# Two layers of Fourier mixing and a spatial-shift MLP: chunk 3's z cast in two halves at later steps, the turns around it moved by one step, and one PSUM copy put ahead of a cast

## The chip, the cores and the metric

The kernel runs on one core of a Trainium2 chip. The metric is device time in microseconds; the kernel before was run three times, and the median counts. A profile of one further execution is read beside it.

The core has a matmul engine (TensorE, PE in the profile, with PEld its weight loads), a vector engine (VectorE, DVE), a scalar engine (ScalarE, ACT), GpSimd (POOL) and SyncE (SP), which in this kernel issues all transfers between HBM and the on-chip memory. Each engine takes its own instructions in the order in which the program emits them, and waits on semaphores for the others. Matmul results land in PSUM, eight banks of 128 x 512 fp32, here named PA, PB, PC and PD with two banks each (psa to psd in the profile).

## The reference

Two layers, each a block A and a block B on x of 2048 x 512, fp32:

```python
def _A_ref(x, dft_seq_re, dft_seq_im, dft_hid_re, dft_hid_im):
    a = jnp.einsum("bsd,ed->bse", x, dft_hid_re)
    b = jnp.einsum("bsd,ed->bse", x, dft_hid_im)
    y = jnp.einsum("ts,bse->bte", dft_seq_re, a) - jnp.einsum("ts,bse->bte", dft_seq_im, b)
    return y

def _B_ref(x, w1, w2, w3, w4):
    h = _gelu(_layernorm(x, axis=-1) @ w1)
    ...
    hs = jnp.concatenate([g0, g1, g2, g3], axis=-1) @ w2
    x1 = x + hs
    h2 = _gelu(_layernorm(x1, axis=-1) @ w3) @ w4
    return x1 + h2

x = x + _A_ref(_layernorm(x, axis=-1), ...)
x = x + _B_ref(_layernorm(x, axis=-1), ...)
```

g0 to g3 are the four quarters of h's columns, shifted along the sequence by +1, -1, +2 and -2 rows.

## The kernel before

**Split numbers.** Every matmul operand is kept as two fp32r numbers, a high part and a low part. `high` (L425) is a ScalarE cast of the fp32 value into the high part, `low` (L428) a VectorE subtraction of the high part from the value. One product of two split operands is three matmuls (`mm3`, L281 to L284): high x high, then the same left side with the right side's low part, then the left side's low part with the right side's high part. So the second or third matmul of a triple can need a low part that the first does not.

**Block A.** The sequence transform goes by chunks c of 512 output rows (four of them); `x_phase` (L475) and `y_phase` (L503) sum the products with the sequence matrices over eight pairs of row tiles. The matrices stream through four raw buffers and a ring of four split buffers: `stage_one` (L215) casts on ScalarE (L228, or L231 and L235 after a subtraction on VectorE), `stage_two` (L239) makes the low part on VectorE (L245). At the last `by1` block of the y phase PC and PD are complete; VectorE makes im0's value from PC (L517) and im1's from re0 and im0 (L520, shown as L468, the line of the helper `add`), ScalarE casts im0 (`high`, L426) and copies PD into X1 (L523). Two blocks of products into PB and PA follow, whose results are copied out at L531 and L533. In the last chunk they go to the tile `beside`, and the hidden transform (`hid`, L550) follows at once in the order of HORDER: its first product takes im0, and its accumulators are PC and PB (`acc4`). For the first three chunks the hidden products are spread over the next chunk's x phase.

**Block B.** `by_pairs` (L714) runs a list of 32 steps, each 12 matmuls of 128 x 128 by 128 x 512. `shifted(c, g)` (L643) multiplies chunk c's transposed normalised rows z (tile zt, halves 0 and 1 over the 512 hidden columns, `z_half`, L711) with column group g of w1; ScalarE applies the gelu into gt (L655) and casts the shifted view into rg (L658, the high part), and VectorE makes its low part (L659). `mixed(c, q)` (L668) multiplies the four groups of rg for one row tile with w2, group order 1, 3, 0, 2, and VectorE adds the result to the tile u (L677). Results rotate through the four banks PD and PA. The steps around the change:

| step | work | step | work |
|---|---|---|---|
| 15, 16, 17 | shifted, chunk 2, groups 1, 3, 0 | 23, 24, 25 | shifted, chunk 3, groups 1, 3, 0 |
| 18 | mixed, chunk 1, tile 3 | 26 | mixed, chunk 2, tile 3 |
| 19 | shifted, chunk 2, group 2 | 27 | shifted, chunk 3, group 2 |
| 20, 21, 22 | mixed, chunk 2, tiles 0 to 2 | 28 to 31 | mixed, chunk 3, tiles 0 to 3 |

**Side work by hand.** All other work of block B is hung on these steps by a schedule written out in the code. `D(n, ...)` puts work behind step n's matmuls and ahead of the step's own ScalarE and VectorE work; `A(n, ...)` puts it behind all of step n (`run`, L735). Within one place the order is that of the calls. A `norm` or `norm3` is a ScalarE normalisation (L330), `ln1_of` another one (four for each chunk, on A of steps 8c+3 to 8c+6, put there first, L844 to L846), `u_stats` the row statistics (VectorE L296 to L300 and two small GpSimd operations), `add_u` a VectorE addition, `turn` and `turn3` 32 x 32 block transposes on VectorE (L594).

To transpose a chunk, its four tiles are turned into a scratch tile (sc0, sc1, sc2), written to HBM by four transfers (`turn_out`, L596) and read back in another view: `turn_in` (L606) brings z into ztf, `b_in` (L696, called by `bring`) brings halves of the second transposed tensor z3d into the blocks "11", "21", "12", "22". The differences of these blocks (`sum_of`), their casts (`highs`) and low parts (`lows`) are operands of the last part of the block, which starts after step 31. Chunk 3's z is read back at A(16) and cast at A(18); its halves' low parts are made at D(21) and D(22). Chunk 1's second turn fills sc2 at D(20) and D(21), is written out at A(21) and read back at A(23); the sum at D(26) is the first use of block "12".

Of the kernel before, what the change touches and what calls it, by code (L numbers as in the profile page):

```python
# [14 lines left out]
S, D, F = 2048, 512, 1376  # L15
# [28 lines left out]
def spectral_mlp_kernel(ctx: ExitStack, tc: tile.TileContext, x, ws, hs, w1, w2, w34, out):  # L44
# [15 lines left out]
    z3d = [dram.tile([D, CH], F32, name=f"z3d{i}") for i in range(NC)]  # L60
# [63 lines left out]
    def xt(j):  # L124
        return xs[j // 2][:, j % 2]
# [29 lines left out]
    def y_order():  # L155
        order = [(k, kind) for k in range(NP) for kind in ("by1", "by0")]
        order[-3], order[-2] = order[-2], order[-3]
        return order
# [111 lines left out]
    def stream():  # L270
        i = state["use"]
        if i and items[i - 1][3] is None:
            state["done"] += 1
        state["use"] += 1
        prefetch()
        while state["two"] <= i:
            stage_two()
        return slots.pop(i)
# [137 lines left out]
    def mm_half(ps, a, slot, first, last):  # L416
        for i in range(2):
            w = slice(i * P, (i + 1) * P)
            mm3(ps[i], a[:, 0, w], a[:, 1, w], slot[:, 0], slot[:, 1], first, last)
# [5 lines left out]
    def high(tf):  # L425
        nc.scalar.copy(tf[0][:, :, 0], tf[1][:, :, 1])  # L426

    def low(tf):  # L428
        nc.vector.tensor_tensor(tf[0][:, :, 1], tf[1][:, :, 1], tf[0][:, :, 0].bitcast(F32), op=ALU.subtract)
# [37 lines left out]
    def add(o, a, b, op=ALU.add):  # L467
        nc.vector.tensor_tensor(o, a, b, op=op)  # L468

    def run_late(*names):  # L470
        for i in names:
            for f in late.pop(i, ()):
                f()
# [29 lines left out]
    def y_phase(c, hook):  # L503
        for k, kind in y_order():
            first, last = k == 0, k == NP - 1
            s = stream()
            if kind == "by1":
                hook(k)
                if k == 2:
                    run_late("y")  # L510
                if k == 4:
                    add(re0s, re0s, im1s)
                mm_half(PC, ay[k][:, 2], s[:, 0], first, last)
                mm_half(PD, ay[k][:, 0], s[:, 1], first, last)
                if last:
                    for i in range(2):
                        nc.vector.scalar_tensor_tensor(  # L517
                            im0s[:, i], PC[i], -1.0, im1s[:, i], op0=ALU.mult, op1=ALU.subtract
                        )
                    add(im1s, re0s, im0s)  # L520
                    high(im0)
                    for i in range(2):
                        nc.scalar.copy(X1[:, i], PD[i])  # L523
            else:
                if k == NP - 2:
                    low(im0)
                mm_half(PB, ay[k][:, 3], s[:, 1], first, last)
                mm_half(PA, ay[k][:, 1], s[:, 0], first, last)
        t = tmp if c < NC - 1 else beside
        for i in range(2):  # L530
            nc.scalar.copy(t[:, i], PB[i])  # L531
        for i in range(2):
            nc.scalar.copy(t[:, 2 + i], PA[i])  # L533
        late.update(
            {
                "im1-": [lambda: add(im1s, im1s, re1s, ALU.subtract)],
                "re1+": [lambda: add(re1s, re1s, t[:, 0:2]), lambda: high(re1)],
                "im1+": [lambda: add(im1s, im1s, X1), lambda: high(im1)],
                "re1": [lambda: low(re1)],
                "re0+": [lambda: add(re0s, re0s, t[:, 0:2])],  # L540
                "im1": [lambda: low(im1)],
                "re0++": [lambda: add(re0s, re0s, t[:, 2:4]), lambda: high(re0)],
                "re0": [lambda: low(re0)],
            }
        )
        if c < NC - 1:
            for i, names in enumerate((["im1-"], ["re1+"], ["im1+", "re1"], ["re0+", "im1"], ["re0++"], ["re0"])):
                late[i + 1] = [f for n in names for f in late.pop(n)]
# [43 lines left out]
    def turn_one(t, q, u):  # L592
        v = t.rearrange("p d (a q j) -> p d a q j", a=NB, q=TC)[:, :, :, q]
        nc.vector.transpose(v, blocks_of(u))  # L594

    def turn_out(t, to=None):  # L596

        if to is None:
            count["turn"] += 1
            to = zd[count["turn"] % 2]  # L600
        z = to.rearrange("(e i) t -> i e t", i=B)
        for b in range(NB):
            v = t[b * B : (b + 1) * B].rearrange("i d (a t) -> i (d a) t", a=NB)
            nc.sync.dma_start(z[:, :, b * P : (b + 1) * P], v)

    def turn_in(dst):  # L606

        z = zd[count["turn"] % 2].rearrange("(d p) t -> p d t", p=P)
        nc.sync.dma_start(dst[:, :, 1], z)
# [86 lines left out]
    def b_in(c, half, to):  # L696
        nc.sync.dma_start(blkf[to][:, :, 1], z3d[c].rearrange("(h d p) t -> h p d t", h=2, p=P)[half])
# [13 lines left out]
    def z_half(c, i):  # L711
        return [t[c % 2][:, 2 * i : 2 * i + 2] for t in (zt, ztf)]

    def by_pairs(layer, zs, xin, dst):  # L714
# [14 lines left out]
        def D(slot, *fs):  # L729
            todo.setdefault((slot, 0), []).extend(fs)  # L730

        def A(slot, *fs):
            todo.setdefault((slot, 1), []).extend(fs)
# [5 lines left out]
        def u_stats(c, i, n=2):  # L739
            return lambda: mrs[c].extend(stats(x1s[c][i : i + n]))  # L740

        def add_u(c, *qs):
            return lambda: [add(xt(c * TC + q), xt(c * TC + q), x1s[c][q]) for q in qs]

        def norm3(c, *qs):
            return lambda: [normed_act(x1s[c][q], x1s[c][q], mrs[c][q]) for q in qs]
# [10 lines left out]
        def turn3(t, c, *qs):  # L757
            return lambda: [turn_one(t, q, x1s[c][q]) for q in qs]
# [4 lines left out]
        def bring(c, half, to):  # L763
            return lambda: b_in(c, half, to)
# [13 lines left out]
        def z_highs(c):  # L778
            return lambda: [high(z_half(c, i)) for i in range(2)]
# [63 lines left out]
        sc0, sc1, sc2 = scratch  # L843
# [27 lines left out]
        D(14, turn(sc1, 3, 2, 3))  # L871
        A(14, lambda: turn_out(sc1))
        A(16, lambda: turn_in(ztf[1]))
        A(18, z_highs(3))
        D(21, lambda: low(z_half(3, 0)))
        D(22, lambda: low(z_half(3, 1)))

        D(6, u_stats(0, 0))
# [15 lines left out]
        D(18, add_u(1, 0, 1, 2))  # L894
        A(19, norm3(1, 0, 1, 2))
        D(19, u_stats(1, 3, 1))
        D(20, add_u(1, 3))
        D(20, turn3(sc2, 1, 0, 1, 2))
        A(20, norm3(1, 3))
        D(21, turn3(sc2, 1, 3))  # L900
        A(21, lambda: turn_out(sc2, z3d[1]))
        A(23, bring(1, 0, "12"), bring(1, 1, "22"))
        A(26, bring(0, 1, "t4"))
        D(26, sum_of("t1", "12", "t1"))
        A(27, highs("12", "22"))
# [538 lines left out]
    for layer in range(LAYERS):  # L1444
# [4 lines left out]
        for c in range(NC):  # L1449
            if layer == 0 and c == 0:  # L1450
# [57 lines left out]
                def hook(i):  # L1508
                    k, odd = divmod(i, 2)
                    if not i:  # L1510
                        second_low(1)
                        xp_stats(1)
                        second_low(0)
                        state["two"] += 1
                        issue_dma()
                        state["limit"] = 4
                        prefetch()
                    state["limit"] = w_items[layer]
                    if not odd:
                        if k + 1 < NP:  # L1520
                            xp_norm(k + 1, 3)
                            xp_main(k + 1)
                        if not k:
                            xp_main_lows(1)
                    else:
                        if 0 < k < NP - 1:
                            xp_main_lows(k + 1)
                        if k + 2 < NP:
                            xp_stats(k + 2)
                        if k:  # L1530
                            xp_sums(k - 1)
                            xp_highs(k - 1, False)
                            xp_lows(k - 1, False)
                    w4_split(i)
# [46 lines left out]
            def hook(k):  # L1581
# [11 lines left out]
                if c == NC - 1 and k == NP - 1:  # L1593
                    turn_in(ztf[0])

            y_phase(c, hook)

        tmps[:] = singles
# [3 lines left out]
        for i, (ri, dp) in enumerate(HORDER):  # L1602
# [17 lines left out]
            if i == 2:  # L1620
                run_late("re0")
                low(z_half(0, 1))
        by_pairs(layer, zs, xin, out if last_layer else x2d)


# [53 lines left out]
```

## Time and profile before

| | us |
|---|---|
| three runs | 1434.35, 1434.81, 1433.13 |
| median | 1434.35 |
| the profiled execution, whole | 1434.7 |
| its span, first to last instruction | 1432.8 |

| engine | busy us | instructions |
|---|---|---|
| VectorE | 1169.5 | 1642 |
| ScalarE | 730.5 | 992 |
| GpSimd | 79.0 | 105 |

The granted TensorE clock was 1.000 over the span. Times in the profile count from the span's start. A row of a timeline gives the start, the duration, the engine, the code line, the operation, the tiles out<-in with their shapes, the number of instructions merged into the row and, in brackets, how long the engine had been idle before it and what ended the wait. Matmuls overlap: each row shows 0.39 us, and the pitch from one start to the next is shorter. A row of the table of waits gives the engine and line that waited, the one that ended the wait, the total in us, the number of times and the longest.

Layer 0 of the two layers spans the first part of the profile, layer 1 the second; the same place of the code appears in both.

### The profile page before, as it was taken

The page shows a single profiled execution, that of the slowest core. Times are in us where ns is not written, and L with a number is a line of the kernel's source. Part 1 is how long each engine was busy: PE and PEld are TensorE (multiplying, and loading weights), DVE is VectorE, ACT ScalarE, POOL GpSimd, SP SyncE. Part 2 cuts the span into 40 slices and gives each one's busy share as a digit, 9 for nine tenths or more (in the row PEclk, how much of TensorE's full clock was granted, in tenths as well). Part 3 has the DMA queues.
Part 4 walks back from the last instruction along what each step waited for, and adds up shares of the span by engine and source line. Part 5 has one row for each costly group of instructions (what it writes and reads, how often), then busy time and mean ns, then how long its engine had stood idle before and what let it go on. Part 6 is the DMA issues. An engine that isn't in the chain of part 4 may idle for free.

```text
span 1432.8 us, 17313 instructions
## 1 busy us (share of the span) xinstructions
PE 1421.6 (99%) x6261; PEld 1173.6 (82%) x6261; DVE 1169.5 (82%) x1642; ACT 730.5 (51%) x992; POOL 79.0 (6%) x105
## 2 busy tenths in 40 slices
PE   9999999999999999999999999999999999999999
PEld 7888888888788788888888888888887878888887
DVE  7986998988979788656789989889988787656676
ACT  5663454455465744434555544544555665343352
POOL 2100000000002000000000000000000020000000
PEclk9999999999999999999999999999999999999999
DMA  7866656657754857944655566575676458477764
GB/s 252 276 206 205 206 192 227 210 184 267 257 162 127 276 193 264 353 157 173 216 166 191 178 233 212 172 246 188 224 273 212 141 162 294 155 244 283 243 205 161
DMA packets 127829, 307.58 MB, mean 215 GB/s; under 512 B 9216, under 2 KB 50176, under 8 KB 124544
## 3 DMA queue, kind: packets, MB, share of 16 engines
q1 hardware_dynamic: 127744, 306.48, 64.5%
q8 instruction: 49, 0.80, 0.2%
q14 instruction: 36, 0.29, 0.1%
HBM read 252.18 MB, written 54.26 MB: 214 GB/s over the span
## 4 chain that ended last, share of the span: by engine, by line
PE 90%; DVE 4%; DMA 3%; ACT 2%; issue 1%; SPq 0%; DVEq 0%; ACTq 0%
PE psd L284 9%; PE psd L282 9%; PE psd L283 9%; PE psa L284 7%; PE psa L283 7%; PE psa L282 7%; PE psc L283 7%; PE psc L284 7%; PE psc L282 7%; PE psb L283 7%; PE psb L282 7%; PE psb L284 7%; DMA raw<-in_ws 2%; DVE ring L245 1%; DMA zt1f<-zd 1%; DMA zd<-scr 1%
## 5 line engine op out<-in xcount | busy, mean ns | idle before, releaser
L228 ACT CAST ring<-raw 128x1024 fp32r<-128x1024 f32 x127 | 132.9, 1053 | 79.0 <-PE psd L284 43.0
L245 DVE TENSOR_TENSOR ring<-raw,ring 128x1024 fp32r<-128x1024 f32 x126 | 153.4, 1219 | 13.9 <-ACT ring L228 13.0
L282 PE MATMUL psd<-ring,rr 128*128 128x512 f32 x208 | 80.9, 389 | 0.0
L283 PE MATMUL psd<-ring,rr 128*128 128x512 f32 x208 | 80.9, 389 | 0.0
L284 PE MATMUL psd<-ring,rr 128*128 128x512 f32 x208 | 80.9, 389 | 0.0
L322 POOL TENSOR_TENSOR rs<-ve,mhalf 128x4 f32<-128x4 f32 x16 | 27.7, 1732 | 607.9 <-DVE nm L321 607.9
L235 ACT CAST ring<-ring0f 128x1024 fp32r<-128x1024 f32 x28 | 29.5, 1054 | 59.7 <-DVE ring0f L234 59.7
L301 POOL TENSOR_TENSOR rs<-ve,mhalf 128x2 f32<-128x2 f32 (+2 forms) x33 | 28.8, 872 | 555.5 <-DVE nb L300 555.5
L619 ACT ACTIVATE tmp<-rest 128x512 f32<-128x512 f32 x30 | 19.0, 632 | 72.9 <-DVE rest L468 72.6
L245 DVE TENSOR_TENSOR ring<-ring1f,ring 128x512 fp32r<-128x512 f32 (+1 forms) x56 | 53.3, 951 | 0.7 <-ACT ring L231 0.7
L283 PE MATMUL psc<-ring,ay 128*128 128x512 f32 x128 | 49.9, 390 | 1.2 <-DVE ring L245 1.2
L283 PE MATMUL psb<-ring,ay 128*128 128x512 f32 x128 | 50.0, 391 | 0.9 <-DVE ring L245 0.9
L330 ACT ACTIVATE tmp<-xs,nb,rs 128x512 f32<-128x512 f32 x56 | 43.3, 809 | 15.1 <-POOL nb L302 13.8
L284 PE MATMUL psb<-ring,ay 128*128 128x512 f32 x128 | 49.8, 389 | 0.0
L284 PE MATMUL psc<-ring,ay 128*128 128x512 f32 x128 | 49.8, 389 | 0.0
L282 PE MATMUL psb<-ring,ay 128*128 128x512 f32 x128 | 49.8, 389 | 0.0
L282 PE MATMUL psc<-ring,ay 128*128 128x512 f32 x128 | 49.8, 389 | 0.0
L235 ACT CAST ring<-ring1f 128x1024 fp32r<-128x1024 f32 x28 | 29.5, 1055 | 38.6 <-DVE ring1f L234 38.6
L282 PE MATMUL psa<-ring,ay 128*128 128x512 f32 x126 | 49.0, 389 | 0.0
L283 PE MATMUL psa<-ring,ay 128*128 128x512 f32 x126 | 49.0, 389 | 0.0
L284 PE MATMUL psa<-ring,ay 128*128 128x512 f32 x126 | 49.0, 389 | 0.0
L282 PE MATMUL psd<-ring,ay 128*128 128x512 f32 x126 | 49.0, 389 | 0.0
(657 smaller groups left out, 4442.2 us busy)
## 6 DMA issues: line engine op xcount, KB each, us to landing
raw<-in_ws SPq DMA_DIRECT2D x183, 512.0 KB, 5.0
w4r<-w4d SPq DMA_DIRECT2D x66, 512.0 KB, 4.7
raw<-in_hs SPq DMA_DIRECT2D x56, 512.0 KB, 3.6
w3b<-w3d SPq DMA_DIRECT2D x14, 1792.0 KB, 7.8
w3d<-w3b SPq DMA_DIRECT2D x5, 1792.0 KB, 6.9
x1d<-tmp SPq DMA_DIRECT2D x12, 512.0 KB, 6.3
xs<-x1d SPq DMA_DIRECT2D x12, 512.0 KB, 5.0
w4d<-w4in SPq DMA_DIRECT2D x11, 512.0 KB, 4.8
```

The source lines that it names most:

```text
L228: nc.scalar.copy(dest[:, a:b, 0], r[0][:, a:b])
L235: nc.scalar.copy(dest[:, :, 0], lo)
L245: nc.vector.tensor_tensor(lo, src, hi.bitcast(F32), op=ALU.subtract)
L282: nc.tensor.matmul(o, lh, rh, start=first, stop=False, skip_group_check=more)
L283: nc.tensor.matmul(o, lh, rl, start=False, stop=False, skip_group_check=more)
L284: nc.tensor.matmul(o, ll, rh, start=False, stop=last, skip_group_check=more)
L301: nc.gpsimd.tensor_tensor(rs[:, :n], ve[:, :n], mhalf[:, 0, :n], op=ALU.pow)
L322: nc.gpsimd.tensor_tensor(rs, ve, mhalf[:, :, :2], op=ALU.pow)
L330: nc.scalar.activation(o, s, AF.Identity, bias=mr[2], scale=mr[1])
L619: nc.scalar.activation(g_of, ps_of, AF.Gelu_apprx_tanh)
```

## The change

Chunk 3's z is no longer cast in one go at A(18), but half 0 at A(19) and half 1 at A(20). The low part of half 0 goes from D(21) to D(20), between the addition and the first three turns of chunk 1. The last turn of chunk 1 goes from D(21) to D(22), behind the low part of half 1, its four writes from A(21) to A(22), and the two reads of it from A(23) to A(24). In the y phase ScalarE's two copies of PD (L523) stand ahead of im0's cast instead of behind it; that place runs once for each chunk but the very first one.

```diff
--- before.py
+++ after.py
@@ -518,9 +518,9 @@
                             im0s[:, i], PC[i], -1.0, im1s[:, i], op0=ALU.mult, op1=ALU.subtract
                         )
                     add(im1s, re0s, im0s)
-                    high(im0)
                     for i in range(2):
                         nc.scalar.copy(X1[:, i], PD[i])
+                    high(im0)
             else:
                 if k == NP - 2:
                     low(im0)
@@ -871,8 +871,8 @@
         D(14, turn(sc1, 3, 2, 3))
         A(14, lambda: turn_out(sc1))
         A(16, lambda: turn_in(ztf[1]))
-        A(18, z_highs(3))
-        D(21, lambda: low(z_half(3, 0)))
+        A(19, lambda: high(z_half(3, 0)))
+        A(20, lambda: high(z_half(3, 1)))
         D(22, lambda: low(z_half(3, 1)))
 
         D(6, u_stats(0, 0))
@@ -894,12 +894,12 @@
         D(18, add_u(1, 0, 1, 2))
         A(19, norm3(1, 0, 1, 2))
         D(19, u_stats(1, 3, 1))
-        D(20, add_u(1, 3))
+        D(20, add_u(1, 3), lambda: low(z_half(3, 0)))
         D(20, turn3(sc2, 1, 0, 1, 2))
         A(20, norm3(1, 3))
-        D(21, turn3(sc2, 1, 3))
-        A(21, lambda: turn_out(sc2, z3d[1]))
-        A(23, bring(1, 0, "12"), bring(1, 1, "22"))
+        D(22, turn3(sc2, 1, 3))
+        A(22, lambda: turn_out(sc2, z3d[1]))
+        A(24, bring(1, 0, "12"), bring(1, 1, "22"))
         A(26, bring(0, 1, "t4"))
         D(26, sum_of("t1", "12", "t1"))
         A(27, highs("12", "22"))
```

`z_highs(c)` calls `high(z_half(c, i))` for i of 0 and 1; no instruction is added or removed.

## The prediction

> **What bounds the kernel now.** I read the page's first part, then the table of waits for TensorE alone, then the timeline of each engine around the two places that the table names.
>
> ```profile
> span 1432.8 us, 17313 instructions
> PE 1421.6 (99%) x6261; PEld 1173.6 (82%) x6261; DVE 1169.5 (82%) x1642; ACT 730.5 (51%) x992; POOL 79.0 (6%) x105
> PE psd L282 <- ACT rg L658: 2.6, 2, 1.4
> PE psc L283 <- DVE ring L245: 1.2, 1, 1.2
> PE psb L282 <- ACT beside L531: 0.4, 1, 0.4
> ```
>
> TensorE is busy 1421.6 of 1432.8 us, so a faster vector or scalar engine is worth only the holes that it closes in TensorE's row. The largest is a wait for the cast of a shifted gelu (L658), once per layer. The wait of L531 is at the other place that the change touches. The wait on L245 is for loads of the sequence matrices, which the change leaves alone.
>
> TensorE in layer 0 and in layer 1 (columns: start, duration, operation, idle before and who ended it):
>
> ```profile
> 465.15 0.39 PE L284 MATMUL psa<-zt,w 128*128 128x512 f32 x1
> 465.38 0.39 PE L282 MATMUL psd<-w,rg 128*128 128x512 f32 x1
> ...
> 467.19 0.39 PE L284 MATMUL psd<-w,rg 128*128 128x512 f32 x1
> 469.03 0.50 PE L282 MATMUL psd<-w,rg 128*128 128x512 f32 x1 [1.45 <-ACT rg L658]
> ...
> 470.10 0.40 PE L282 MATMUL psd<-w,rg 128*128 128x512 f32 x1
> ```
>
> ```profile
> 1177.26 0.39 PE L284 MATMUL psd<-w,rg 128*128 128x512 f32 x1
> 1178.83 0.50 PE L282 MATMUL psd<-w,rg 128*128 128x512 f32 x1 [1.18 <-ACT rg L658]
> ...
> 1179.89 0.39 PE L282 MATMUL psd<-w,rg 128*128 128x512 f32 x1
> ```
>
> 465.38 is the first matmul of step 20 (mixed of chunk 2), 467.19 its ninth: 1.81 over 8, a pitch of 0.227 us. The tenth needs group 2 of chunk 2, which step 19 has only just made. It starts at 469.03, and the three after the hole are slow too; the thirteenth (first of step 21) is due at 467.19 + 4 x 0.227 = 468.10 and comes at 470.10. The hole costs **2.00 us**, more than the 1.45 of idle time. In layer 1: 1177.26 + 0.91 = 1178.17 against 1179.89, **1.72 us**.
>
> Why the cast is late, on ScalarE:
>
> ```profile
> 465.48 2.13 ACT L426 CAST zt<-zt1f 128x1024 fp32r<-128x1024 f32 x2 [4.01 <-DMA zt1f<-zd]
> 467.51 0.19 ACT L654 COPY gt<-gt 128x2 f32<-128x2 f32 x1
> 467.73 0.60 ACT L655 ACTIVATE gt<-psa 128x512 f32<-128x512 f32 x1
> 468.36 0.62 ACT L658 CAST rg<-gt 128x512 fp32r<-128x512 f32 x1
> 468.88 0.81 ACT L330 ACTIVATE tmp<-xs,nb,rs 128x512 f32<-128x512 f32 x1
> 469.61 2.22 ACT L330 ACTIVATE rest<-rest,nb,rs 128x512 f32<-128x512 f32 x3
> 475.50 1.04 ACT L426 CAST b<-b21f 128x1024 fp32r<-128x1024 f32 x1
> ```
>
> Both halves of chunk 3's z are cast at the end of step 18. ScalarE stood 4.01 us for their DMA and then cast for 2.13 us, while step 19's product was ready at 465.15 + 0.39 = 465.54. The gelu waits behind the z casts, and TensorE behind the gelu.
>
> **The change part by part.** *The z casts (steps 18 to 19 and 20).* Nothing is added: two casts move behind the gelu. With nothing in front, the gelu starts at about 465.6 (465.54 and a semaphore), and its cast, from 467.73 to 468.36 + 0.62 = 468.98 in the rows, takes 1.25: done at 466.9. The tenth matmul is due at 467.42, so it has 0.5 to spare. The twelfth needs the low half as well:
>
> ```profile
> 469.01 0.69 DVE L659 TENSOR_TENSOR rg<-gt,rg 128x512 fp32r<-128x512 f32 x1 [3.05 <-ACT rg L658]
> ...
> 470.44 2.13 DVE L594 STREAM_TRANSPOSE scr<-rest 128x512 f32<-128x512 f32 x3
> 472.49 0.65 DVE L677 TENSOR_TENSOR tmp<-psd,tmp 128x512 f32<-128x512 f32 x1
> 473.07 1.20 DVE L429 TENSOR_TENSOR zt<-zt1f,zt 128x1024 fp32r<-128x1024 f32 x1
> 474.19 0.70 DVE L594 STREAM_TRANSPOSE scr<-rest 128x512 f32<-128x512 f32 x1
> ```
>
> VectorE stood idle 3.05 us before this subtraction, so it runs as soon as the cast is done: 466.9 + 0.69 = 467.6, due at 467.42 + 0.45 = 467.87. Both margins are positive, so the whole hole closes: **2.00 + 1.72 = 3.72 us**.
>
> *What is late next.* ScalarE has the same work from 465.5 to 476.54 (475.50 + 1.04), only in another order: gelu and cast, one normalisation (0.81), half 0 of z (half of 2.13), three normalisations (2.22), one more, half 1. With the overlaps of these rows half 0 is cast by 468.6 and half 1 by 472.4. VectorE then does: low of half 0 from 468.6, 1.20; three turns, 2.13; two adds of 0.65; low of half 1, 1.20; the last turn, 0.70. End to end that is 475.1; the rows overlap by about 0.08 (470.44 + 2.13 against 472.49), which makes low of half 1 end at 474.2 and the last turn at 474.8. TensorE reaches step 23 two steps of 12 x 0.227 after 468.10, at 473.54, and its eighth matmul is the first that reads low of half 1: 475.13. That is 0.6 to 0.9 to spare, so I cost it at nothing; without that cover it is one to one. The last turn was done at 474.19 + 0.70 = 474.89, so the transfers behind it start when they did, while TensorE is 2 us earlier. In layer 1, where the hole is 0.28 smaller, the same sum gives an end 0.17 later than before.
>
> *The moved transfers.* The four writes of z3d[1] go out at step 22 and the two reads of it at step 24. On SyncE's queue nothing stands between the old places and the new ones (t1's read stays ahead, the next w3 load behind), so their order is kept and the first write is set by the last turn. The tight place is layer 1:
>
> ```profile
> 1184.71 3.11 SPq L604 DMA_DIRECT2D z3d<-scr  x4
> 1191.31 0.38 SPq L697 DMA_DIRECT2D b12f<-z3d  x1
> ```
>
> ```profile
> DMA to landing us min/median/max: 3.6/4.0/4.6
> ```
>
> ```profile
> 1195.68 1.22 DVE L468 TENSOR_TENSOR bt1f<-b12f,bt1f 128x1024 f32<-128x1024 f32 x1
> ...
> 1200.50 0.69 DVE L659 TENSOR_TENSOR rg<-gt,rg 128x512 fp32r<-128x512 f32 x1 [1.24 <-ACT rg L658]
> ```
>
> The middle row is the view of tile b12f: issue to landing. Writes from 1184.88 put the read at 1191.48 and its landing at 1195.1 to 1196.1. The sum t1 waits for it at the head of VectorE, and behind it are an add, the statistics of chunk 2 and the low half (L659) of step 27, which TensorE wants for step 28. From the sum's start to VectorE being free took 1200.50 - 1.24 - 1195.68 = 3.58, so free at 1198.7 to 1199.7. L659 itself could run at 1200.50 - 1.72 = 1198.78. By step 20's margins (467.6 against 467.87) it may be 0.2 late for nothing: a cost of 0 to 0.7 us; I take 0, since the landing of 3.6 is the one seen nearest, in this stage.
>
> *PD's copies before im0's cast.* Layer ends, TensorE first, then ScalarE:
>
> ```profile
> 389.80 0.39 PE L284 MATMUL psc<-ring,rr 128*128 128x512 f32 x1
> ...
> 390.86 0.40 PE L284 MATMUL psb<-ring,rr 128*128 128x512 f32 x1
> ```
>
> ```profile
> 1099.58 0.39 PE L284 MATMUL psc<-ring,rr 128*128 128x512 f32 x1
> ...
> 1100.93 0.40 PE L284 MATMUL psb<-ring,rr 128*128 128x512 f32 x1
> ```
>
> ```profile
> 383.00 0.39 PE L284 MATMUL psd<-ring,ay 128*128 128x512 f32 x1
> ```
>
> ```profile
> 385.84 1.05 ACT L426 CAST rr<-rr10f 128x1024 fp32r<-128x1024 f32 x1 [2.26 <-DVE rr11f L468]
> 386.80 1.07 ACT L523 COPY tmp<-psd 128x512 f32<-128x512 f32 x2
> 387.75 2.01 ACT L228 CAST ring<-raw 128x1024 fp32r<-128x1024 f32 x2
> 389.65 1.08 ACT L531 COPY beside<-psb 128x512 f32<-128x512 f32 x2
> ```
>
> Three matmuls of 0.227 after 389.80 is 390.48, it came at 390.86: 0.38 lost; 1100.26 against 1100.93: 0.67. TensorE waits for bank PB, whose copy (L531) stands behind im0's cast, PD's copies and two ring casts. PD is finished at 383.39 and ScalarE idles 2.26 us before im0's cast, from 383.58: PD's copies (1.07) fit into that idle time with 1.2 to spare. Everything behind them moves up by 387.75 - 386.80 = 0.95, L531 to 388.70, its first half done by 389.3, while TensorE wants the bank at 390.03. So **0.38 + 0.67 = 1.05 us**. Bounds: 0 if the ring casts cannot start earlier (their loads or slots), 1.05 otherwise; I take 1.05, as they ran without a wait of their own.
>
> Before, no such copy ran beside VectorE's reads of PC; if the two shared a port and VectorE lost the whole 1.07:
>
> ```profile
> 386.92 1.23 DVE L429 TENSOR_TENSOR rr<-rr10f,rr 128x1024 fp32r<-128x1024 f32 x1
> ```
>
> ```profile
> 389.12 0.39 PE L284 MATMUL psc<-ring,rr 128*128 128x512 f32 x1
> ```
>
> then im0's low half would end at 388.15 + 1.07 = 389.22, wanted at 389.12: 0.1 per layer, and not less than 0. The Trainium skill (PSUM — Partial Sum Buffer, Specifications) says that ScalarE and VectorE read it side by side at full bandwidth in different banks; by that rule this term is 0, as I take it, and no run here shows it yet.
>
> **Sum.** 3.72 + 1.05 = 4.77. Span 1432.8 - 4.8 = 1428.0. The profiled execution took 1434.7, 1.9 above its span, so 1429.9; the median 1434.35 is 0.35 under that execution: **1429.6 us**.
>
> **Rivals.** *R1, the turn's transfers become the next wait*: b12's landing takes 4.6 and step 28 loses up to 0.7, with some restart cost: 1430.4. For it: the chain from the last turn to b12 keeps its clock time while TensorE comes earlier. Against: margin in layer 0, where no statistics stand behind the sum. *R2, the PD copies give nothing*, since the ring casts wait for loads: 1429.6 + 1.05 = 1430.6. Against: no idle is shown before L228 at 387.75. *R3, the z casts move the hole instead of closing it*: if half 0 is cast only after the three normalisations, VectorE is 2.1 later, low of half 1 ends near 476.4 and step 23 stands 1.2 plus 0.3 of slow restart in each layer: 1429.6 + 3.0 = 1432.6, within the noise. For it: ScalarE has no idle time in this stretch. Against: the cast is appended ahead of them. *R4, slower*: PD's copies now stand at the head of ScalarE and hold im0's cast. Place: both layer ends. Up to 1.4 us of lateness (copies starting 384.8 instead of 383.4) nothing happens, the next 0.97 (389.12 - 388.15) is covered too, then TensorE stands one to one; above 2.4 + 1.9 = 4.3 us of lateness each the 3.72 is eaten. At 5 us late: 1434.35 - 3.72 + 2 x 2.6 = 1435.8. Against: PD's end at 383.39. The Trainium skill (TensorE: Matmul & The Clock Gate, the paragraph on engine queue depths) has ScalarE's queue as strictly first in, first out; that rule is what would make R4 work, and the 2.13 us gelu delay above agrees with it.
>
> **Chances.** Forecast 0.56, R1 0.12, R2 0.12, R3 0.12, R4 0.04, and 0.04 for a slower case that I do not see. A change under 0.2% (2.9 us) cannot be told from none here. Forecast, R1 and R2 are faster by more than that: 0.80; R3 is within: 0.13; slower 0.07. The runs before spread over 1.7 us, so the forecast's own range is 1428.6 to 1430.6; with the gains of R1 and R2 lost together and part of R3, up to 1432.2; below, 1428.3 allows for fewer late loads.
>
> **What would show it.** Right: no wait of L282 on rg L658 in the table; step 20 at pitch 0.227 in both layers; the z casts after L658 of step 19; L523 before L426 at each layer end and no wait on beside L531. Wrong: a new wait of TensorE on zt L429 at step 23 (R3), on rg L659 at step 28 (R1), on rr L429 or L426 at the layer's end (R4), or L228 idle until a load (R2).

## The result and the profile after

| | before | after |
|---|---|---|
| median, us | 1433.94 (1432.57 to 1434.81, 6 runs) | 1429.24 (1427.48 to 1429.75, 6 runs) |
| profiled execution, us | 1434.7 | 1429.24 |
| its span, us | 1432.8 | 1427.3 |

The ratio of after to before is 0.9966, 95% interval 0.9956 to 0.9976: 4.7 us faster by the medians, 3.4 to 6.3 us by the interval. The forecast was 1429.6 within 1428.3 to 1432.2, with 4.77 us worked out. Three more runs took the median of the kernel before from 1434.35 to 1433.94, which is about the 0.36 us by which the time came out under the forecast. That the gain agrees within 0.1 us is in part luck, since the interval is 2.9 us wide; the traces below carry the account.

The first part of the page after, and the table of waits for TensorE (engine and line that waited, line that ended it; total us, times, longest):

```profile
span 1427.3 us, 17317 instructions
PE 1420.0 (99%) x6261; PEld 1173.8 (82%) x6261; DVE 1168.8 (82%) x1642; ACT 732.1 (51%) x992; POOL 79.7 (6%) x105
```

```profile
...
PE psb L283 <- DVE ring L245: 0.4, 1, 0.4
PE psc L283 <- DVE ring L245: 0.3, 1, 0.3
PE psa L282 <- ACT rr00f L501: 0.3, 1, 0.3
```

Both waits that the change was aimed at, on rg L658 and on beside L531, are gone, and no new name from block B or from the layer ends has come in. What is left are waits at the kernel's start (left out above) and, in the y phase of the last chunk, waits for the ring and one for ScalarE's copy of re0 (L501). Step 20 of layer 0 now, TensorE, ScalarE and VectorE (start, duration, operation, idle before; left-out rows are marked by dots):

```profile
464.03 0.39 PE L282 MATMUL psd<-w,rg 128*128 128x512 f32 x1
...
465.85 0.39 PE L284 MATMUL psd<-w,rg 128*128 128x512 f32 x1
466.07 0.39 PE L282 MATMUL psd<-w,rg 128*128 128x512 f32 x1
...
466.53 0.40 PE L284 MATMUL psd<-w,rg 128*128 128x512 f32 x1
```

```profile
464.29 0.60 ACT L655 ACTIVATE gt<-psa 128x512 f32<-128x512 f32 x1 [4.08 <-PE psa L284]
464.92 0.62 ACT L658 CAST rg<-gt 128x512 fp32r<-128x512 f32 x1
...
466.17 1.03 ACT L426 CAST zt<-zt1f 128x1024 fp32r<-128x1024 f32 x1
...
469.94 1.03 ACT L426 CAST zt<-zt1f 128x1024 fp32r<-128x1024 f32 x1
```

```profile
465.58 0.69 DVE L659 TENSOR_TENSOR rg<-gt,rg 128x512 fp32r<-128x512 f32 x1 [0.97 <-ACT rg L658]
...
467.23 1.23 DVE L429 TENSOR_TENSOR zt<-zt1f,zt 128x1024 fp32r<-128x1024 f32 x1 [0.36 <-ACT zt L426]
468.37 1.89 DVE L594 STREAM_TRANSPOSE scr<-rest 128x512 f32<-128x512 f32 x3
...
471.36 1.21 DVE L429 TENSOR_TENSOR zt<-zt1f,zt 128x1024 fp32r<-128x1024 f32 x1
472.49 0.70 DVE L594 STREAM_TRANSPOSE scr<-rest 128x512 f32<-128x512 f32 x1
```

The tenth matmul follows the ninth at pitch (465.85, 466.07). ScalarE's wait in front of the gelu is now for TensorE's product; before, its 4.01 us were for the transfer of z, which landed at 465.48, just when the product was ready (465.54). So it was the two casts of 2.13 us in front of the gelu that made it late, and not the wait for the transfer. The cast ends at 464.92 + 0.62 = 465.54, 0.53 ahead of the tenth matmul, and the low half at 466.27, 0.26 ahead of the twelfth.

The layer end of layer 0, ScalarE and then TensorE:

```profile
382.80 1.06 ACT L522 COPY tmp<-psd 128x512 f32<-128x512 f32 x2
385.16 1.06 ACT L426 CAST rr<-rr10f 128x1024 fp32r<-128x1024 f32 x1 [1.30 <-DVE rr11f L468]
386.12 2.00 ACT L228 CAST ring<-raw 128x1024 fp32r<-128x1024 f32 x2
388.02 1.05 ACT L531 COPY beside<-psb 128x512 f32<-128x512 f32 x2
```

```profile
388.98 0.39 PE L284 MATMUL psc<-ring,rr 128*128 128x512 f32 x1
389.21 0.39 PE L282 MATMUL psb<-ring,rr 128*128 128x512 f32 x1
```

PD's copies (L522 in this kernel) sit in what was idle time, and im0's cast still waits only for VectorE. The copies of PB begin 1.19 ahead of the matmul that wants the bank, where before the first of them ended after it was wanted.

The next table adds up every start of a matmul that comes later than the pitch, from the first chunk to the tail, as worked out from the two traces. It includes the restarts, which are the slow starts right behind a hole.

```
                                   before   after
step 20, layer 0 and layer 1       2.00 + 1.72    0
layer ends                         0.46 + 0.74    0
last chunk's y phase               0.90 + 2.05    0.11 + 2.05
other                              0.42    0.42
sum                                8.29    2.58
```

(The layer ends hold 0.08 each, at the second product, that the prediction left out.) 8.29 - 2.58 = 5.7, of which 0.8 are ring waits of layer 0 that this execution did not have. They go from 0 to 1.3 us in the profiles of the experiments. Of the whole change only the copies run ahead of this place, and with the copies alone they came to 1.3, so I do not count them as its gain. Of the 2.05 after, 0.57 stand behind the copy of re0. The spans differ by 5.5; the part that the change took is 4.9.

### The profile page after: what moved, and what is told of

Read it like the earlier page. It is cut to its first block, busy times and chain, and to the rows that moved or that the text cites. A ratio compares the mean times of both kernels' runs of the same rounds, so it can differ in the third digit from the quotient of the medians.

```text
span 1427.3 us, 17317 instructions
## 1 busy us (share of the span) xinstructions
PE 1420.0 (99%) x6261; PEld 1173.8 (82%) x6261; DVE 1168.8 (82%) x1642; ACT 732.1 (51%) x992; POOL 79.7 (6%) x105
## 4 chain that ended last, share of the span: by engine, by line
PE 96%; DVE 2%; DMA 2%; issue 0%; SPq 0%; ACT 0%; DVEq 0%
PE psd L283 10%; PE psd L282 10%; PE psd L284 10%; PE psa L283 8%; PE psa L282 8%; PE psa L284 8%; PE psc L283 7%; PE psc L284 7%; PE psc L282 7%; PE psb L283 7%; PE psb L282 7%; PE psb L284 7%; DMA raw<-in_ws 2%; DVE ring L245 1%; DVE ring2f L234 0%
## 5 line engine op out<-in xcount | busy, mean ns | idle before, releaser
L282 PE MATMUL psa<-ring,ay 128*128 128x512 f32 x126 | 49.2, 390 | 0.3 <-ACT rr00f L501 0.3
L283 PE MATMUL psa<-ring,ay 128*128 128x512 f32 x126 | 49.1, 389 | 0.0
L282 PE MATMUL psd<-ring,ay 128*128 128x512 f32 x126 | 49.0, 389 | 0.0
L283 PE MATMUL psd<-ring,ay 128*128 128x512 f32 x126 | 49.0, 389 | 0.0
```

The lines of the kernel that those rows point to most:

```text
L282: nc.tensor.matmul(o, lh, rh, start=first, stop=False, skip_group_check=more)
L283: nc.tensor.matmul(o, lh, rl, start=False, stop=False, skip_group_check=more)
```

## The experiments

Each kernel was timed beside the kernel before (the one with six copies has a single execution); ratios are to that kernel, with their 95% interval, and holes are read from the profiled execution. Distances from the kernel after are differences of medians that were not taken side by side. The median of the kernel before went from 1433.47 to 1434.3 between these sets of runs, so such a distance is known to some 0.8 us only.

**The copies alone.** The kernel before with only this:

```diff
-                    high(im0)
                     for i in range(2):
                         nc.scalar.copy(X1[:, i], PD[i])
+                    high(im0)
```

> The kernel before with the y phase edit alone: PD's copies ahead of im0's cast, block B untouched. Theory (two independent holes, each closed by its own edit): 1.05 us faster than before, from the two waits on the copy of PB at the layer ends (0.38 and 0.67), with both waits on the shifted gelu's cast left at 2.00 and 1.72 us. Rival (the copies give nothing, all of the gain is block B's): 0.0 us, and a wait on L531 still in the table.

Measured: 1432.9 us against 1433.47, ratio 0.9994 (0.9985 to 1.0003). The time alone does not settle 1.05 us. The table of waits does:

```profile
PE psd L282 <- ACT rg L658: 2.8, 2, 1.4
...
PE psb L283 <- DVE ring L245: 0.7, 1, 0.7
...
```

The wait on beside L531 is gone and the one on rg L658 is there in both layers. So the holes at the layer ends close by this edit alone. That they are worth 1 us of time is read from the trace; the timed gain is 0.57 with an interval from 2.2 faster to 0.4 slower, which holds 1.05 as well as 0.

**Block B alone.** The kernel after with the copies put back.

```diff
-                    for i in range(2):
-                        nc.scalar.copy(X1[:, i], PD[i])
                     high(im0)
+                    for i in range(2):
+                        nc.scalar.copy(X1[:, i], PD[i])
```

> The kernel after with the y phase edit undone: the z casts, turns and transfers moved, PD's copies behind im0's cast. Theory: 3.7 us faster than before (2.00 + 1.72), no hole at step 20, the two holes at the layer ends back at about 0.4 and 0.7 us. Rival (the copies carry part of block B's gain, because what follows a layer end then starts in another rhythm): under 3.0 us faster, with part of the hole at step 20 left.

Measured: 1429.66 us against 1433.47, ratio 0.997 (0.9959 to 0.9982): 3.8 us, where 3.7 was expected. Step 20 has no hole. At the layer ends the matmul that takes PB comes late again, by 0.40 and 0.65 with its restart; its wait is back in the table:

```profile
PE psb L282 <- ACT beside L531: 0.4, 1, 0.4
```

The two halves of the change are independent, and block B's is the larger.

**The casts without the moves around them.**

```diff
-        A(18, z_highs(3))
+        A(19, lambda: high(z_half(3, 0)))
+        A(20, lambda: high(z_half(3, 1)))
```

> The kernel before with the two z casts alone moved (half 0 to A(19), half 1 to A(20)); low parts, turns and transfers where they were, y phase as before. Theory (the hole at step 20 belongs to the casts, the other moves keep VectorE from being late at step 23): no hole at step 20, so 2.00 + 1.72 us won, but low of half 1 now stands behind the last turn and the add of step 21 and ends about 0.4 us after TensorE asks for it at step 23: a new hole of 0.2 to 0.8 us in each layer, so 2.1 to 3.3 us faster than before. Rival (the moved turns and transfers are part of what closes the hole): step 20 still stands more than 0.5 us in a layer. Second rival (the moved turns change nothing): 3.7 us faster and no new hole.

Measured: 1431.62 us against 1433.47, ratio 0.9985 (0.9976 to 0.9993): 1.9 us, a little under the lower end of what was expected (1.0 to 3.4 by the interval). Step 20 has no hole. VectorE and TensorE at step 23:

```profile
474.42 1.21 DVE L429 TENSOR_TENSOR zt<-zt1f,zt 128x1024 fp32r<-128x1024 f32 x1
```

```profile
474.70 0.40 PE L282 MATMUL psa<-zt,w 128*128 128x512 f32 x1
475.68 0.50 PE L283 MATMUL psa<-zt,w 128*128 128x512 f32 x1 [0.58 <-DVE zt L429]
```

The low half of z ends at 475.63 and TensorE, which was due at 474.93, starts at 475.68: 0.75 late and 0.11 of restart, 0.86 us; in layer 1 the same sum is 0.92. So the casts alone close the hole at step 20 and open one at step 23: 3.72 - 0.86 - 0.92 = 1.94. Putting half 0's low part ahead of the turns and the last turn behind half 1's, with its transfers, is what keeps VectorE ahead of step 23; these moves were not tried one by one. Both rivals fall: step 20 does not need the moves, and the moves are not idle.

**Half 0 cast behind the normalisations.** The kernel after with the order inside A(19) turned round: this is R3 of the prediction by itself.

```diff
-        A(19, lambda: high(z_half(3, 0)))
         A(19, norm3(1, 0, 1, 2))
+        A(19, lambda: high(z_half(3, 0)))
```

> The kernel after with half 0's cast put behind the three normalisations of A(19) in place of ahead of them. Theory: step 20 has no hole, but VectorE waits about 2.1 us longer for half 0, low of half 1 ends about 1 us after TensorE asks for it at step 23, and each layer stands 0.9 to 1.5 us there: 1.8 to 3.0 us slower than the kernel after, 1.7 to 2.9 us faster than before. Rival (VectorE has more slack than reckoned): within 0.5 us of the kernel after.

Measured: 1431.44 us against 1433.47, ratio 0.9985 (0.9976 to 0.9994): 2.0 us faster than before and 2.2 us above the kernel after. Both lie in what was expected.

```profile
470.04 1.22 DVE L429 TENSOR_TENSOR zt<-zt1f,zt 128x1024 fp32r<-128x1024 f32 x1 [2.49 <-ACT zt L426]
```

```profile
474.26 0.39 PE L282 MATMUL psa<-zt,w 128*128 128x512 f32 x1
475.42 0.50 PE L283 MATMUL psa<-zt,w 128*128 128x512 f32 x1 [0.77 <-DVE zt L429]
```

VectorE stands 2.49 us in place of 0.36 for half 0, and the hole at step 23 is 1.05 us with its restart in each layer (due at 474.26 + 0.23 = 474.49). A further 0.3 us is lost later in each layer, at step 26 in layer 0 and at step 28 in layer 1. In layer 0 VectorE's row shows no wait between half 0 and the low half that is late there, so its lateness has travelled on.

**The read of block 12 one step later still.** R1 of the prediction, with a lateness that TensorE must feel.

```diff
-        A(24, bring(1, 0, "12"), bring(1, 1, "22"))
...
             A(25, lambda: w3_load(1))
...
+        A(25, bring(1, 0, "12"), bring(1, 1, "22"))
```

> The kernel after with the two reads of z3d[1] moved one step further, to A(25), where in layer 0 they stand behind the load of the next w3 pieces on SyncE's queue; in layer 1 no such load is there. Theory (the prediction's R1 as a mechanism: a late block 12 holds the sum t1 at the head of VectorE and through it the low half that step 28 needs): in layer 0 the read goes out near 483.9 in place of 479.6, lands near 487.5, and TensorE stands 1.6 to 2.4 us at the twelfth matmul of step 28; in layer 1 nothing changes. 1.5 to 2.5 us slower than the kernel after. Rival (there is slack enough behind the sum): no hole at step 28, within 0.5 us of the kernel after.

Measured: 1433.24 us against 1434.3, ratio 0.9993 (0.9983 to 1.0003): 4.0 us above the kernel after, more than expected. SyncE, VectorE and TensorE in layer 0:

```profile
483.46 0.39 SPq L814 DMA_DIRECT2D staged<-in_w  x1
484.03 0.38 SPq L697 DMA_DIRECT2D b12f<-z3d  x1
```

```profile
488.84 1.23 DVE L468 TENSOR_TENSOR bt1f<-b12f,bt1f 128x1024 f32<-128x1024 f32 x1 [4.84 <-DMA b12f<-z3d]
...
490.59 0.68 DVE L659 TENSOR_TENSOR rg<-gt,rg 128x512 fp32r<-128x512 f32 x1
```

```profile
488.16 0.39 PE L283 MATMUL psd<-w,rg 128*128 128x512 f32 x1
491.32 0.65 PE L284 MATMUL psd<-w,rg 128*128 128x512 f32 x1 [2.78 <-DVE rg L659]
491.77 0.63 PE L282 MATMUL psd<-w,rg 128*128 128x512 f32 x1
```

The mechanism is as expected: the read stands behind the w3 load, the sum behind the read, the low half (L659) behind the sum, and the twelfth matmul of step 28 behind the low half. Layer 1 has no such hole. Its size was off twice. The read took 4.8 us to land in place of 3.6, so the twelfth matmul is 2.94 late in place of 1.6 to 2.4. And the nine starts behind it come at 0.32 to 0.45, most of them at 0.43, in place of 0.227: 1.7 us more.

**More copies of PD.** In the last chunk's y phase PD is copied three and five times over.

```diff
-                    for i in range(2):
-                        nc.scalar.copy(X1[:, i], PD[i])
+                    for i in range(2 if c < NC - 1 else 6):      # or 10
+                        nc.scalar.copy(X1[:, i % 2], PD[i % 2])
```

> The kernel after with PD copied three times over (six copies in place of two, the same values) in the last chunk's y phase alone. They take about 1.9 us longer; in the kernel after ScalarE idles 1.30 us before im0's cast and im0's low half is 0.82 us early, 2.1 us together. Theory (the cover reckoned for R4 is real): no hole above 0.3 us at either layer end. Rival (PD's copies are on the path already): 1 us or more per layer end.

> The same with ten copies, about 3.8 us longer. Theory: 3.8 - 2.1 = 1.7 us of hole at the first products of im0 at each layer end (1.4 to 2.3 with slow restarts and the later copy of PB), so 2.8 to 4.6 us slower than the kernel after, waits on rr L429 in TensorE's table. Rival (more cover than reckoned): under 1 us in all.

Six copies: one execution, 1428.19 us; nothing at im0's first products, and at most 0.3 us at a later product of a layer end. ScalarE with six, then with ten:

```profile
382.45 3.02 ACT L522 COPY tmp<-psd 128x512 f32<-128x512 f32 x6
385.32 1.10 ACT L426 CAST rr<-rr10f 128x1024 fp32r<-128x1024 f32 x1
```

```profile
383.23 4.97 ACT L522 COPY tmp<-psd 128x512 f32<-128x512 f32 x10
388.00 1.13 ACT L426 CAST rr<-rr10f 128x1024 fp32r<-128x1024 f32 x1
```

Ten copies: 1432.74 us against 1434.3, ratio 0.9991 (0.9982 to 1.0001), 3.5 us above the kernel after; TensorE waits twice at each layer end:

```profile
389.19 0.50 PE L282 MATMUL psc<-ring,rr 128*128 128x512 f32 x1 [0.94 <-ACT rr L426]
...
390.45 0.50 PE L284 MATMUL psc<-ring,rr 128*128 128x512 f32 x1 [0.52 <-DVE rr L429]
```

With six the idle time in front of im0's cast is used up and im0's products do not wait. With ten the cast comes 4.77 us after the copies' start, in the kernel after 2.36 (385.16 - 382.80), so 2.4 later, and TensorE loses 2.5 and 2.1 us at the two ends. The ten copies take 3.9 us longer than two (4.97 - 1.06); with the cover of 2.1 that was worked out for this test, 1.8 are left. TensorE's two waits make it late by 1.10 and 0.69 at the end of layer 0, 1.8 together, and by 0.74 and 0.69 at that of layer 1; the rest of the loss are restarts and a small later hole. So the cover is real, and beyond it the copies cost about what they take, plus the restarts.

**Two tries at a faster version.** The ring waits of the last chunk's y phase are what remains. The four writes of the transposed z one at each of blocks 2 to 5:

```diff
-                if c == NC - 1 and k == 2:
-                    turn_out(turned0)
+                if c == NC - 1 and 2 <= k < 2 + NB:
+                    turn_write(turned0, k - 2)
```

(`turn_write` issues one of the four transfers of `turn_out`.)

> A try at a version that beats both: the kernel after with the four writes of the transposed z in the last chunk's y phase issued one at each of blocks 2 to 5 in place of all four at block 2, so that the loads of the sequence matrices behind them on SyncE's queue are not held up together. The late loads cost 0.9 and 2.0 us in the profile before, 0.1 and 2.1 us in the profile after. If the writes hold the loads up: up to 2 us faster than the kernel after. If the loads are late for other reasons (the buffers come free late, the transfers are slow): within 0.5 us of it. If the writes now reach the read-back of z too late: a wait at the layer end, slower.

And the four block transposes one at each of blocks 0 to 3, with the writes at block 4:

```diff
-                if c == NC - 1 and k == 0:
-                    for q in range(TC):
-                        turn_one(turned0, q, tmp[:, q])
-                if c == NC - 1 and k == 2:
+                if c == NC - 1 and k < TC:
+                    turn_one(turned0, k, tmp[:, k])
+                if c == NC - 1 and k == TC:
                     turn_out(turned0)
```

> A second try at a version that beats both: the kernel after with the four block transposes of the last chunk's y phase done one at each of blocks 0 to 3 in place of all at block 0, and their four writes at block 4. In the profile after VectorE makes all four in one row of 2.49 us at the start of this phase in layer 1, and TensorE loses 0.57 and 0.70 us around it waiting for the ring. If that burst is what is late: those two holes go, 0.5 to 1.5 us faster than the kernel after. If the loads themselves are late: within 0.5 us of it.

Measured: 1429.7 us (ratio to before 0.9968, 0.9957 to 0.9979) and 1429.84 us (0.9972, 0.9959 to 0.9984), both within 0.6 of the kernel after. The waits moved rather than went. In the second the hole of 0.70 that it was aimed at is gone, the one of 0.57 (0.61 here) is not, and those further on in the phase are larger. The tables of waits of the two, first and second:

```profile
PE psc L283 <- DVE ring L245: 2.3, 2, 1.3
```

```profile
PE psc L283 <- DVE ring L245: 1.8, 2, 1.0
```

The chain of waits of the second shows one of its holes (start, duration, what):

```profile
369.74 6.13 DMA raw<-in_ws
...
376.00 1.23 DVE ring1f L234
377.22 1.15 DVE ring L245
...
378.41 0.50 PE psc L283
```

In that chain the load goes out as soon as VectorE is done with a subtraction (L234, until 369.35), and takes 6.13 us to land; in the first kernel the same chain has 6.40 us. So spreading the writes or the transposes did not take these waits away. Whether VectorE's row or the slow transfer is the better place to start was not settled; nothing here beats the kernel after.

## Why the prediction was right, point by point

**The hole at step 20** (3.72 us): right in mechanism and size. What made the gelu late were the two casts themselves: the transfer that ScalarE had waited for landed when step 19's product was ready. The gelu now starts as soon as its product is there, the margins came out at 0.53 and 0.26 where 0.5 and 0.27 were worked out, and block B alone gives 3.8 us (2.6 to 5.9 by the interval).

**What is late next**: right in sign. The margin at step 23 was worked out as 0.6 to 0.9 (its own sum, end to end, gives 0.7 for the lower bound). In layer 0 the low part of half 1 ends at 471.36 + 1.21 = 472.57:

```profile
473.81 0.39 PE L283 MATMUL psa<-zt,w 128*128 128x512 f32 x1
```

That is the eighth matmul, 1.24 later. The term that was mis-sized is the row of three turns, taken at 2.13 us; that row of before held a wait for the third normalisation, and without it three turns take 1.89. The last turn therefore ended 9.16 us after the start of step 20 (473.19 - 464.03) in place of 9.42. The experiment with the casts alone shows that the order matters: with the same work in the old order VectorE is 0.75 us too late.

**R1**, the turn's transfers: its wait is there, its price is not. VectorE in layer 1 of the kernel after:

```profile
1190.71 1.22 DVE L468 TENSOR_TENSOR bt1f<-b12f,bt1f 128x1024 f32<-128x1024 f32 x1 [0.64 <-DMA b12f<-z3d]
...
1194.81 0.69 DVE L659 TENSOR_TENSOR rg<-gt,rg 128x512 fp32r<-128x512 f32 x1 [0.51 <-ACT rg L658]
```

The sum now stands 0.64 us for block 12, and VectorE is still free 0.51 us before L659 can run. The prediction took 0 and it is 0. It had the read of layer 1 at 1191.48, which is 1187.48 in the time of this trace (step 20 starts 4.00 us earlier); it went out at 1187.03, partly because the last turn ended earlier, and it took the 3.6 us to land that the prediction had chosen. With the longest landing of this tile here, 4.4 us, VectorE would have been some 0.3 us late by an estimate from these rows, about the margin that step 20 showed, so the choice of 3.6 decided little. The read one step later shows that a late block 12 does reach TensorE, and that a hole of 2.94 us there cost 1.7 us more than itself.

**The copies** (1.05 us): right by the trace, both holes gone with the edit and back without it. The whole change came out 0.42 us faster than block B alone by the medians (0.9 if each is taken against the runs of the kernel before beside it: 4.7 and 3.8), and the copies alone 0.57 faster than before. Neither difference is resolved, so the timed size stays open: the interval of the copies alone holds nothing as well as 1.05. What the prediction bounded at 0.1 us a layer, VectorE's reads of PC slowed by the copies beside them, did not happen. Its row in the kernel before, and in the kernel after:

```profile
383.27 1.28 DVE L517 SCALAR_TENSOR_TENSOR rr10f<-psc,rr11f 128x512 f32<-128x512 f32 x2
```

```profile
382.59 1.28 DVE L517 SCALAR_TENSOR_TENSOR rr10f<-psc,rr11f 128x512 f32<-128x512 f32 x2
```

The row takes 1.28 us in both, in the second with L522 running beside it from 382.80. The Trainium skill (PSUM — Partial Sum Buffer, Specifications) says that the two engines read different banks side by side at full bandwidth; this row agrees.

**R2** fell: the ring casts moved up with the copies (386.12, right behind im0's cast). **R3**, tried by itself, costs 2.2 us where 3.0 were worked out: 1.05 us a layer at step 23 in place of 1.5, since VectorE was earlier than reckoned, and 0.3 a layer of late consequences. **R4** fell, and its cover was measured: with six copies the layer ends lose at most 0.3 us, with ten 2.1 to 2.5 us each. The prediction had put the cover at 2.4 us; the rows of the kernel after give 2.1 (1.30 of idle time in front of im0's cast and 0.82 by which its low half is early).

## What to carry to other kernels

On a bound engine with 99% busy time, look at what stands in the queue in front of the one instruction that it waits for: work put ahead of work whose input is just ready delays it by its own length (2.13 us of casts here), and by what is left of a wait for a transfer in front of it (here next to nothing, as the transfer landed just then). Moving it a step behind costs nothing as long as its own user is far enough away. Such a move is finished only when the next user's queue has been reckoned through: the casts alone gave back 1.8 of 3.7 us at step 23. A copy out of PSUM can go into the first idle time behind its last matmul, ahead of work that still waits for another engine, as long as it fits: here two copies did and six still did, ten did not.

## What the runs showed of the hardware

A hole in TensorE's row costs more than its idle time, in one case here much more. After idle times of 0.4 to 1.5 us the next one to three starts came at 0.33 to 0.39 us. After the 2.78 us of the late read of block 12 the clock itself fell (columns of this view of that kernel: stretch, its length, busy time of TensorE, weight loads, VectorE, ScalarE and GpSimd with their counts, granted clock, DMA share, GB/s):

```profile
...
491.30:495.00 3.70, 3.68 (x9) 2.90 (x10) 2.87 (x3) 3.13 (x4) 0.00 (x0) 0.54 0.99 348
495.00:503.00 8.00, 8.00 (x36) 6.60 (x36) 7.64 (x9) 3.80 (x5) 0.00 (x0) 1.00 0.75 304
```

The granted clock was 0.54 over 3.7 us and then 1.00 again. The Trainium skill (TensorE: Matmul & The Clock Gate, Part 1) states a half-rate clock after an idle window of about 3.4 us. Here it followed an idle time of 2.78 us, which is shorter, in the one case of these runs; an idle time of 1.45 us was followed by a granted clock of 1.00. Where between the two the clock falls was not tried.
